# Row maxima as the exponential's bias, half products from chunk 8 on, and a new order, in a fused window-attention and gated-FFN kernel

## The chip, the cores and the metric

The kernel runs on one core of one Trainium2 chip. The metric is the device time of one launch in microseconds (us), as the median of three runs. Five engines work side by side, each through its own queue in order: TensorE (PE; its weight loads are listed apart, as PEld), VectorE (DVE), ScalarE (ACT), GpSimd (POOL), and SyncE (SP), which here only issues DMAs.

## The reference, cut to what matters

```python
# attention: 8 batches, 8 heads, 576 positions, 64 wide; key j counts for query i if 0 <= i - j < 64
scores = scale * np.matmul(q, k.transpose(0, 1, 3, 2))
scores = np.where(mask, scores, -1000000000.0)
scores = scores - np.max(scores, axis=-1, keepdims=True)
attn = np.exp(scores)
attn = attn / (np.sum(attn, axis=-1, keepdims=True) + 1e-09)
x = np.matmul(attn, v)              # then read as 4608 tokens of 512
# gated FFN: 512 -> 2048 -> 512
h = x @ w_in
sp = np.maximum(h, 0.0) + np.log1p(np.exp(-np.abs(h)))
out = (h * erf(sp)) @ w_out
```

## The kernel before

The 4,608 tokens are cut into 36 **units** of 128 tokens for the attention and 18 **chunks** of 256 tokens (two units each) for the FFN. Numbers are split into a high and a low float16 part, and a product is made of three float16 products (high·high, high·low, low·high).

**Attention of a unit** u. `s` (`scores`) makes the scores of all heads in PSUM, even heads in one bank, odd heads in the other ("parity" 0 and 1). `m` (`masked_max`) adds the mask and takes the row maxima, on DVE: four instructions of 128x128 for a parity, one for each head, each with an accumulator read that writes one column of `rmx`, a part of the tile `small`. `f` (`shift`) then subtracts the maxima from the 128x512 scores of the parity, on DVE or POOL; `e` (`expo`) takes the exponential on ACT, 128x512 at once from unit 6 on, with a constant bias; `ph` and `r` split it into high and low part, `t` transposes it by DMA, `a` multiplies by V on PE, `n` normalizes. Units 0 to 5 take another way through `tp` (a transpose on PE).

**FFN of a chunk** c. It is worked in two halves g (two numbers g for a chunk, from g = 2c). The first product is direct for chunks 0 to 3 (`mm`, line 763), and from chunk 4 on made of seven products of half-size blocks in place of eight (`M`, line 807), for which `U`, `Uh`, `Ul` (lines 791 and 797) prepare sums of weight blocks and `T`, `yh`, `yl` sums of x blocks. `E` and `C` bring the results from PSUM to the tile `h`; `sp`, `er`, `gt` are softplus, erf and the gate (`gt`: line 845, from chunk FAST on line 843). The second product is direct up to chunk FAST-1: `gh`, `gl` split the gated tile, `mA` and `mB` (`mm2`, line 869) multiply 128x512 at a time: per chunk 2 halves x 2 x 2 x 4 x 3 = 96 matmuls. From chunk FAST on it, too, is made of seven half products: `A` and `B` (lines 575/577 and 936) split a quadrant, `S` adds quadrants on an engine or by an accumulating DMA (lines 943 and 941), `P` and `Q` (`fast`, line 957) make 7 x 2 x 4 x 3 = 168 matmuls of 128x256 per chunk, `O` clears a bank, and `K` and `J` write the results out. Its weight sums are prepared once, by `Z`, `Yh`, `Yl` (lines 899 to 913).

**The order** is written out by hand: PLAN is one list of tokens (`m:7:0` is unit 7, parity 0; a letter at the end names the engine, v = DVE, a = ACT, g = POOL). The program issues them in that order, so each engine's queue is the list cut down to its tokens. FAST sets two more limits, LONE = FAST-3 and LENT = FAST-2, the chunks up to which some spare tiles serve another purpose.

Of the kernel before, what the change touches and what calls it, by code (L numbers as in the profile page):

```python
# [44 lines left out]
FAST = 7  # L45
# [236 lines left out]
def window_attention_gated_ffn(ctx, tc, q, k, v, w_in, w_out, masks, out):  # L282
# [6 lines left out]
    def fixed(name, shape, dt=F32):  # L289
        return const.tile(shape, dt, name=name)  # L290
# [778 lines left out]
```

## Time and profile before

| | |
|---|---|
| median of 3 runs | 837.74 us (837.42 to 838.18) |
| the profiled execution | 837.51 us, span of its instructions 835.6 us |
| mean granted TensorE clock | 0.998 |
| busy share of the span | PE 97%, PEld 81%, DVE 89%, ACT 76%, POOL 47% |

The span is the time from the first to the last instruction of the profiled execution; its own time is 1.9 us longer. A busy share says how much of the span an engine spent in instructions. Matmuls are pipelined, so that a busy PE is not a PE at its peak; a DVE or POOL instruction counts as busy also while it is held up by another engine.

### The profile page before, as it was taken

The numbers are of one execution on the slowest core, as the hardware profiler recorded it, in microseconds if no ns is written. First come the engines' busy times: TensorE is split into PE (matmuls) and PEld (weight loads), VectorE is DVE, ScalarE is ACT, GpSimd is POOL, SyncE is SP. The second block draws the span as 40 slices with busy tenths as digits, with TensorE's granted clock in tenths as the row PEclk, the third lists the DMA queues.
The fourth block names the chain that finished last, engine by engine and source line by source line (L and its number), as shares of the span: only waits on it lengthen the run. The fifth ranks groups of instructions, "written<-read, shape, count | busy, mean of one in ns | idle before, by whom it ended". The sixth has DMA issues, their size and how long they took to land.

```text
span 835.6 us, 26675 instructions
## 1 busy us (share of the span) xinstructions
PE 807.7 (97%) x11358; PEld 674.1 (81%) x11358; DVE 742.5 (89%) x1617; ACT 631.4 (76%) x833; POOL 396.8 (47%) x371
## 2 busy tenths in 40 slices
PE   7898989999999999999999999999999999999998
PEld 7786757656677775767889998989898989999997
DVE  5899999999998989889998989998879899887677
ACT  4798988778879888688758685868787858764673
POOL 1243445341644865353337367645554643723352
PEclk9999999999999999999999999999999999999999
DMA  9974485580476769162628595747774644522002
GB/s 351 361 279 166 127 218 147 101 196 2 108 162 163 151 144 179 46 153 51 120 49 176 113 179 102 157 89 180 118 153 96 154 90 91 90 49 61 9 5 73
DMA packets 148663, 109.87 MB, mean 131 GB/s; under 512 B 123456, under 2 KB 123840, under 8 KB 148544
## 3 DMA queue, kind: packets, MB, share of 16 engines
q1 hardware_dynamic: 145808, 98.60, 49.2%
q0 software_dynamic: 2592, 9.44, 6.3%
q8 instruction: 89, 1.46, 0.7%
q14 instruction: 30, 0.25, 0.1%
q10 hardware_dynamic: 144, 0.13, 0.0%
HBM read 59.64 MB, written 9.44 MB: 83 GB/s over the span
## 4 chain that ended last, share of the span: by engine, by line
PE 62%; DVE 24%; ACT 7%; issue 3%; POOL 2%; DMA 2%; DVEq 0%; SPq 0%; ACTq 0%; POOLq 0%
PE hp L807 23%; PE o L957 19%; PE o L869 11%; PE s L501 3%; PE hp L763 3%; PE av L557 2%; DVE y L845 2%; DVE y L843 2%; DVE w L421 2%; DVE h L936 1%; ACT y L831 1%; DVE vs L421 1%; DVE qk L512 1%; DVE h L823 1%; DVE sm L512 1%
## 5 line engine op out<-in xcount | busy, mean ns | idle before, releaser
L957 PEld LDWEIGHTS <-h 128*128 128x128 f16 x1632 | 155.8, 98 | 27.1 <-DVE h L936 5.6
L807 PE MATMUL hp<-arena,w 128*128 128x128 f16 x2688 | 162.4, 219 | 0.4 <-DVE h L823 0.4
L807 PEld LDWEIGHTS <-w 128*128 128x128 f16 x2688 | 154.8, 98 | 5.9 <-issue 1.2
L807 PE MATMUL hp<-arena 128*128 128x128 f16 x2016 | 119.7, 219 | 0.8 <-DVE h L823 0.7
L807 PEld LDWEIGHTS <-arena 128*128 128x128 f16 x2016 | 114.5, 98 | 4.0 <-issue 2.0
L957 PE MATMUL o<-w,h 128*128 128x256 f16 x912 | 108.8, 273 | 1.9 <-DVE h L936 1.3
L575 ACT ACTIVATE h<-hp 128x512 f32<-128x512 f32 x109 | 63.9, 588 | 42.9 <-PE hp L807 34.1
L763 PE MATMUL hp<-arena,w 128*128 128x256 f16 (+1 forms) x960 | 90.2, 252 | 2.1 <-DVE w L421 1.6
L936 POOL TENSOR_TENSOR h<-y,h 128x512 f16<-128x512 f32 x48 | 64.1, 1341 | 52.3 <-ACT h L575 20.5
L763 PEld LDWEIGHTS <-w 128*128 128x128 f16 x960 | 78.0, 98 | 13.4 <-DVE w L421 2.5
L831 ACT ACTIVATE y<-h,c 128x1024 f32<-128x1024 f32 x72 | 80.3, 1142 | 6.1 <-DVE h L823 4.4
L575 ACT ACTIVATE h<-y 128x512 f16<-128x512 f32 x84 | 50.1, 622 | 38.0 <-DVE y L943 14.6
L936 DVE TENSOR_TENSOR h<-y,h 128x512 f16<-128x512 f32 x88 | 70.2, 818 | 8.2 <-ACT h L575 4.2
L869 PE MATMUL o<-w,gh 128*128 128x512 f16 x320 | 74.7, 379 | 1.0 <-ACT gh L414 0.5
L838 ACT ACTIVATE y<-y 128x1024 f32<-128x1024 f32 x72 | 74.6, 1052 | 0.5
L823 DVE TENSOR_TENSOR h<-hp,h 128x512 f32<-128x512 f32 x84 | 57.6, 686 | 19.0 <-PE hp L807 14.7
L843 DVE SCALAR_TENSOR_TENSOR y<-h,small,y 128x1024 f32<-128x1024 f32 x44 | 58.2, 1327 | 4.3 <-ACT y L838 3.7
L869 PEld LDWEIGHTS <-gh 128*128 128x128 f16 x320 | 30.0, 98 | 34.2 <-issue 1.1
L957 PE MATMUL o<-spare,h 128*128 128x256 f16 x460 | 55.6, 273 | 1.0 <-DVE h L936 0.6
L838 ACT ACT_TABLE_LOAD x43 | 55.2, 1283 | 0.7
L517 POOL TENSOR_TENSOR sm<-sm,small 128x512 f32<-128x512 f32 x26 | 33.0, 1273 | 30.7 <-DVE small L512 21.4
L501 PE MATMUL s<-kr,qr 64*64 64x128 f32 x1152 | 40.7, 279 | 5.2 <-DMA kr<-k_in 4.7
(255 smaller groups left out, 1675.6 us busy)
## 6 DMA issues: line engine op xcount, KB each, us to landing
vr<-v_in SPq DMA_DIRECT2D x36, 520.0 KB, 4.4
kr<-k_in SPq DMA_DIRECT2D x36, 384.0 KB, 4.1
qr<-q_in SPq DMA_DIRECT2D x36, 256.0 KB, 4.0
y<-y POOLq DMA_DIRECT2D x18, 512.0 KB, 5.1
out<-ob SPq DMA_DIRECT2D x33, 256.0 KB, 3.3
w<-w_in SPq DMA_DIRECT2D x4, 1024.0 KB, 8.0
arena<-w_in SPq DMA_DIRECT2D x4, 1024.0 KB, 9.1
arena<-w_out SPq DMA_DIRECT2D x4, 1024.0 KB, 4.8
```

The source lines that it names most:

```text
L501: nc.tensor.matmul(sps[par][t, i, :], qx[rows, i, t], kx[rows, i, W * blk:W * blk + P], start=n == 0, stop=n == len(terms) - 1)
L517: eng_of(eng).tensor_tensor(s, s, m.unsqueeze(2).broadcast_to([P, HP, P]), op=ALU.subtract)
L575: nc.scalar.activation(dst, src, AF.Copy)
L763: nc.tensor.matmul(hps[pc % 2][:, f, at_t], w1[a][hf][:, cc, fs], xt[b][c % 2][:, cc:2 * NCC:NCC, :][:, at_x, :], start=(n == 0), stop=(n ...
L807: nc.tensor.matmul(bank[:, q, f, :], left(m, a, 2 * hf + q)[:, cc, f * P:(f + 1) * P], xt[b][c % 2][:, slot + cc, :], start=m in (1, 2, 5) ...
L823: nc.vector.tensor_tensor(dst, bank_view(1), dst, op=ALU.add)
L831: nc.scalar.activation(at(yb, g, n), at(hb, g, n), AF.Softplus, scale=st_c[g][:, n:n + 1])
L838: nc.scalar.activation(y, y, AF.Erf)
L843: nc.vector.scalar_tensor_tensor(y, at(hb, g, n), gain(g, n), y, op0=ALU.mult, op1=ALU.mult)
L869: nc.tensor.matmul(ops[j], a[:, f // 2, j, f % 2, :], w2[b][:, hf * GF + n * GF // 2 + f, :], start=n == 0 and f == 0 and a is gh and b == ...
L936: eng_of(eng).tensor_tensor(lo, quadrant(m)[:, 512 * h:512 * (h + 1)], hi, op=ALU.subtract)
L957: nc.tensor.matmul(dst, a[:, at_f], right(m, n, 2 * h + f // 2)[:, f % 2], start=False, stop=f == 3 and (a is lo or n == 1), skip_group_ch ...
```

## The change

From unit 6 on `f` is gone. A new step `nb` (`max_bias`) turns both parities' maxima of a unit at once (128x8) into -max/8 + 14 ln 2, and `e` takes the raw masked scores with that as bias. The bias is one column for each head, so a parity's exponential is four instructions of 128x128. FAST goes from 7 to 8: chunk 7's second product is direct, and ten chunks are left on half products (LONE and LENT follow). The tile `small` grows from 68 to 84 columns. PLAN is a new list.

```diff
-FAST = 7
+FAST = 8
 LONE = FAST - 3
 LENT = FAST - 2
...
-    small = fixed("small", [P, 68])
+    small = fixed("small", [P, 84])
...
-    rmx = [few(HP) for _ in range(4)]
+    mxs, nmx = ([few(2 * HP) for _ in range(2)] for _ in range(2))
+    rmx = [mxs[i // 2][:, i % 2 * HP:i % 2 * HP + HP] for i in range(4)]
...
+    def max_bias(u, eng):
+        if eng == "a":
+            nc.scalar.activation(nmx[u % 2], mxs[u % 2], AF.Identity, bias=shift14, scale=-0.125)
+            return
+        eng_of(eng).tensor_scalar(nmx[u % 2], mxs[u % 2], -0.125, LN14, op0=ALU.mult, op1=ALU.add)
...
-        nc.scalar.activation(s, s, AF.Exp, bias=shift14, scale=0.125 if u >= LATE else es)
+        if u >= LATE:
+            for j in range(HP):
+                nc.scalar.activation(s[:, j, :], s[:, j, :], AF.Exp, bias=nmx[u % 2][:, HP * par + j:HP * par + j + 1], scale=0.125)
+            return
+        nc.scalar.activation(s, s, AF.Exp, bias=shift14, scale=es)
...
-    "ph:6:1:g m:7:0 c:13 r:6:1:v py:3 e:6:0 mm:2:2 pc:3 gl:0:1 ph:6:0:a vh:6:a t:6:0 d:13 r:6:0:v mB:0:1:0 vh:7:g t:6:1 "
+    "gt:0:1 h:6:a n:4 s:6 gh:0:1:a gl:0:0 a:5:0 c:13 a:5:1 xh:4:g m:6:1 mm:2:1 lv:7 xl:4:g m:6:0 l:11 nb:6:a e:6:0 l:7 "
```

Of the tokens, 60 `f` go (39 of them on POOL, 21 on DVE) and 30 `nb` come (13 on ACT, 9 on DVE, 8 on POOL); chunk 7 loses 14 each of `P`, `Q`, `A`, `B`, 4 `S`, 3 `K`, 3 `J` and 2 `O`, and gains 8 `mA`, 8 `mB`, 4 `gh`, 4 `gl` and 2 `fo`. Among the tokens that stay, engines are dealt anew: DVE takes 12 more `pk` (a maximum over 128x512), 5 more `E` and 6 more `Uh`, POOL takes 6 more `Z`, 7 more `ph` and 5 more `xl` but 11 fewer `B`. Counted over the whole program, POOL's instructions with two input tiles (TENSOR_TENSOR) go from 207 to 169; those that stand in the list ahead of chunk 4's first product from 42 to 29, and those from chunk 9's first product on from 105 to 78.

On ACT, around the exponentials of unit 6 (tiles sm0 and sm1; h is filled from PSUM between them, p is the high part), before:

```order
L838 ACTIVATE y1_108<-y1_108 128x1024
L537 ACT_TABLE_LOAD
L537 ACTIVATE sm1_96<-sm1_96,small_65 128x512
L575 ACTIVATE h0_105<-hp1_116 128x512
L652 ACTIVATE arena_61<-arena_61 128x1024
L537 ACTIVATE sm0_95<-sm0_95,small_65 128x512
L575 ACTIVATE p0_0_97<-sm0_95 128x512
```

and now (line 541 is `expo`, line 513 `nb`, line 581 the copies of line 575):

```order
L658 ACTIVATE arena_61<-arena_61 128x1024
L513 ACTIVATE small_65<-small_65 128x8
L541 ACTIVATE sm0_95<-sm0_95,small_65 128x128 x4
L581 ACTIVATE h0_105<-hp0_115 128x512
L541 ACTIVATE sm1_96<-sm1_96,small_65 128x128 x4
L581 ACTIVATE p0_0_97<-sm0_95 128x512
```

Each exponential is four instructions, and `nb` stands ahead of them.

On POOL, in the stretch of units 6 and 7, two steps `U` (line 791) and the subtractions (line 517) stood before:

```order
L418 TENSOR_SCALAR w1_01_100<-w2_0_103,small_65 128x2x512
L791 TENSOR_TENSOR misc_76<-w1_00_99 128x512
L791 TENSOR_TENSOR misc_76<-misc_76,w1_10_101 128x512
L517 TENSOR_TENSOR sm1_96<-sm1_96,small_65 128x512
L517 TENSOR_TENSOR sm0_95<-sm0_95,small_65 128x512
L577 CAST p0_0_97<-sm1_96 128x512
L418 TENSOR_SCALAR spare_89<-vr1_88,csc_67 128x16x64
```

These first two `U` now stand on DVE (line 797), among the low parts of the weights (line 417) and small scales:

```order
L417 SCALAR_TENSOR_TENSOR w2_1_104<-w1_01_100,small_65,w2_0_103 128x1024
L797 TENSOR_TENSOR misc_76<-w1_00_99 128x512
L417 SCALAR_TENSOR_TENSOR w2_1_104<-w1_11_102,small_65,w2_0_103 128x1024
L583 COPY h1_106<-hp0_115 128x512
L405 TENSOR_SCALAR csc_67<-cpw_66 128x3
L748 TENSOR_SCALAR c1_77<-small_65,cpw_66 128x2
L797 TENSOR_TENSOR misc_76<-misc_76,w1_10_101 128x512
```

The subtractions are gone from POOL there, and the two `U` moved to DVE.

On PE, chunk 7's second product began after a product `M` (line 807) with half products of 128x256:

```order
L807 LDWEIGHTS arena_61
L807 MATMUL hp0_115<-arena_61 128x128
L957 LDWEIGHTS h1_106
L957 MATMUL o0_117<-w2_0_103,h1_106 128x256
L957 LDWEIGHTS h1_106
L957 MATMUL o0_117<-w2_1_104,h1_106 128x256
```

and now ends, ahead of such a product (line 813), with direct ones of 128x512 (line 875):

```order
L875 LDWEIGHTS h1_106
L875 MATMUL o1_118<-w2_0_103,h1_106 128x512
L875 LDWEIGHTS h1_106
L875 MATMUL o1_118<-w2_1_104,h1_106 128x512
L813 LDWEIGHTS arena_61
L813 MATMUL hp0_115<-arena_61 128x128
```

Chunk 7 went from 168 narrow matmuls to 96 of twice the width.

## Rows read from the trace of the kernel before

**Rows 1.** The page: its first line, and the busy time of each engine.
```profile
span 835.6 us, 26675 instructions
PE 807.7 (97%) x11358; PEld 674.1 (81%) x11358; DVE 742.5 (89%) x1617; ACT 631.4 (76%) x833; POOL 396.8 (47%) x371
```

**Rows 2.** Busy time of each engine in three stretches, with its columns' line.
```profile
core 0: us, PE busy (x) PEld busy (x) DVE busy (x) ACT busy (x) POOL busy (x), PEclk, DMA share, GB/s
95.00:190.00 95.00, 90.22 (x974) 62.22 (x973) 92.19 (x222) 77.06 (x99) 43.85 (x38) 0.98 0.68 159
190.00:400.00 210.00, 208.42 (x2696) 147.36 (x2695) 192.24 (x435) 173.86 (x238) 103.71 (x85) 1.00 0.54 116
400.00:836.00 436.00, 426.13 (x6418) 394.79 (x6415) 376.44 (x707) 307.31 (x400) 217.28 (x206) 1.00 0.52 103
```

**Rows 3.** The chain that ended last, 95 to 190 us: start, length, instruction.
```profile
98.45 1.18 DVE arena L577
...
100.84 1.98 DVE y L845
...
104.57 1.14 DVE y L845
...
115.48 1.05 DVE cmx L406
...
141.53 0.94 DVE small L726
...
149.63 0.17 DVE cmx L406
```

**Rows 4.** The chain that ended last, two long pieces on PE after 190 us.
```profile
348.12 8.63 PE o L869 x40
...
719.07 10.48 PE o L957 x96
```

**Rows 5.** ACT's groups by shape: busy, mean ns of one, idle before.
```profile
L537 ACT ACTIVATE sm<-sm,small 128x512 f32<-128x512 f32 x31 | 21.9, 715 | 3.7 <-DVE sm L517 3.5
...
L414 ACT ACTIVATE ob<-o,sg 128x256 f32<-128x256 f32 x19 | 8.9, 470 | 20.0 <-PE o L957 18.3 <-DVE ob L977 1.7
L834 ACT ACTIVATE small<-small 128x1 f32<-128x1 f32 x36 | 7.2, 200 | 0.6
```

**Rows 6.** Line 517, the subtraction: shortest, median, longest, in ns.
```profile
L517 POOL TENSOR_TENSOR sm<-sm,small x26: 1037/1042/2022, 7.7 to 612.0; 128x512 f32<-128x512 f32 x26
...
L517 DVE TENSOR_TENSOR sm<-sm,small x13: 673/682/1096, 8.5 to 684.1; 128x512 f32<-128x512 f32 x13
```

**Rows 7.** DVE in order of time, two stretches: start, length, instruction.
```profile
100.76 2.06 DVE L845 TENSOR_TENSOR y<-h,y 128x1024 f32<-128x1024 f32 x1
...
182.04 0.68 DVE L517 TENSOR_TENSOR qk<-qk,small 128x512 f32<-128x512 f32 x1
...
186.90 1.64 DVE L517 TENSOR_TENSOR qk<-qk,small 128x512 f32<-128x512 f32 x1
```

**Rows 8.** POOL in order of time, beside those; idle before in brackets.
```profile
99.73 2.01 POOL L517 TENSOR_TENSOR spare<-spare,small 128x512 f32<-128x512 f32 x1
...
115.45 1.04 POOL L517 TENSOR_TENSOR qk<-qk,small 128x512 f32<-128x512 f32 x1 [2.47 <-DVE cmx L447]
...
185.93 2.06 POOL L791 TENSOR_TENSOR arena<-arena,w 128x512 f32<-128x512 f32 x1 [5.14 <-DVE arena L791]
```

**Rows 9.** Line 517 on POOL, from 95 to 190 us alone.
```profile
L517 POOL TENSOR_TENSOR sm<-sm,small x6: 1037/1042/1892, 97.5 to 177.8; 128x512 f32<-128x512 f32 x6
...
L517 POOL TENSOR_TENSOR qk<-qk,small x4: 1037/1042/1045, 115.5 to 147.6; 128x512 f32<-128x512 f32 x4
L517 POOL TENSOR_TENSOR spare<-spare,small x1: 2006/2006/2006, 99.7 to 99.7; 128x512 f32<-128x512 f32 x1
```

**Rows 10.** Line 791, the steps `U`, on DVE: shortest, median, longest.
```profile
L791 DVE TENSOR_TENSOR misc<-misc,w x9: 677/683/694, 123.3 to 246.8; 128x512 f32<-128x512 f32 x9
```

**Rows 11.** PE in order of time, in chunk 7's half products.
```profile
418.88 0.72 PE L957 MATMUL o<-gh,h 128*128 128x256 f16 x5 [1.72 <-DVE h L936]
```

**Rows 12.** PE's weight loads waiting, 420 to 836 us: total, times, longest.
```profile
PEld L957 <- DVE h L936: 3.3, 6, 1.1
PEld L957 <- DVE h L577: 1.7, 4, 0.6
...
PEld L957 <- ACT h L575: 0.9, 2, 0.7
```

More of the change, by code (lines that the diff above doesn't have):

```diff
@@ L1002, in window_attention_gated_ffn @@
         "qh": q_hi, "ql": q_lo, "kh": k_hi, "kl": k_lo, "vh": v_hi, "vl": v_lo, "s": scores, "m": masked_max,
-        "f": shift, "tp": upend, "e": expo, "ph": expo_hi, "r": expo_rest, "t": turn, "a": weigh, "n": normalize, "xp": x_up, "xh": x_hi, "xl": x_lo,
+        "f": shift, "nb": max_bias, "tp": upend, "e": expo, "ph": expo_hi, "r": expo_rest, "t": turn, "a": weigh, "n": normalize, "xp": x_up, "xh": x_hi, "xl": x_lo,
         "xt": x_turn, "T": x_sums, "yh": odd_hi, "yl": odd_lo, "yt": odd_turn, "U": sum_step, "Uh": sum_hi, "Ul": sum_lo, "M": product, "E": take, "C": join, "L": fetch, "d": low_bits, "c": rebias, "o": assemble,
```

433 rows, old and new, of the table PLAN are left out of this document.

## The prediction

> **What bounds the kernel now.** I read the page first. PE is busy for 97% of the span and DVE for 89%; ACT has a quarter of the span free and POOL half [rows 1]. That names PE, but an average hides stages, so the next view is the chain that ended last, read against the busy time by stretch. From 95 to 190 us the chain runs mostly from one DVE instruction to the next, and DVE is busy for 92.19 of these 95 us while PE has 4.8 us free [rows 2, 3]. From 190 to 400 us PE is busy for 208.42 of 210 us, and the chain is made of long PE pieces [rows 2, 4]. From 400 us to the end PE is free for 9.9 of 436 us, some 4 of them after its last matmul [rows 2]. So there are two regimes: DVE sets the pace for about a tenth of the run, then PE does, with small waits in the stage of the half products. Time is won or lost in three ways only: PE's own work anywhere after 190 us, DVE's pace before, and PE's small waits behind 400 us. All that PE waits for in 95 to 836 us is 4.8 + 1.6 + 9.9 = 16.3 us; no new order can win more than that.
>
> **PE's work: up.** Chunk 7's second product was 168 matmuls of 128x256; 96 in a row took 10.48 us, 0.109 each, so 18.3 us. It becomes 96 of 128x512; 40 took 8.63 us, 0.216 each, so 20.7 us [rows 4]. That is **+2.4 us** in the regime where PE is the bound, with nothing to hide it. The two bank clears that go are single small matmuls; I count them as nothing.
>
> **DVE's work: dealt out again, not less.** The 21 subtractions that leave DVE take 0.68 us each, 14 us [rows 6]. But DVE takes over 12 maxima of 128x512, 5 copies from PSUM and 6 casts from other engines; at the same 0.68 us these 23 are 16 us. Over the whole run I take that as even, and none of it counts in the PE regime. In the DVE regime there is something to count: until unit 12 every subtraction stood on POOL, so DVE loses none there, while two steps U come from POOL to DVE among the weights' low parts. At 0.683 us [rows 10] they are **+1.4 us** of DVE's queue. The bound below is nothing (if DVE happens to wait just there), the one above is these 1.4 us.
>
> **POOL's work: what it holds up.** 39 subtractions of at least 1.04 us, 41 us in all, leave POOL [rows 6], which is not a bound. But POOL holds DVE up. The gate at 100.76 us took 2.06 us and 1.98 of the chain, against 1.14 on the chain for the same instruction at 104.57 [rows 3, 7]: a subtraction ran on POOL from 99.73 to 101.74 [rows 8], and the gate ended about one own length after it. The small mask at 115.48 took 1.05 us against 0.17 at 149.63 [rows 3]; a subtraction on POOL ran from 115.45 to 116.49 [rows 8]. POOL ran 11 subtractions from 95 to 190 us [rows 9]; I find five DVE instructions held by them, the first at 98.45 and the last at 141.53 [rows 3], by 0.4 to 0.9 us against the shortest of their kind, 3.7 us in sum. All 11 go. In their place POOL has three more steps U ahead of chunk 4's first product; such a step held a DVE instruction for 0.96 us (1.64 against 0.68, at 186.90) [rows 7, 8]. With the share that was held before, five in eleven, three steps cost 3 x 5/11 x 0.9 = 1.2 us. I take 3.7 - 1.2 = **-2.5 us**; the bounds are nothing (POOL's other work slides into the free slots) and -3.7.
>
> The Trainium skill says the same of the cause (GPSIMD Engine Reference, Specifications): POOL's SBUF interfaces are shared with VectorE, with contention for DVE instructions that have two SBUF inputs or run in a two-port mode. The gate, with two inputs, agrees. The page gives no price; by it alone the sign of this term would be as above.
>
> **The first half products.** In chunk 7, where they begin, PE waits 1.72 us for a DVE split of line 936 [rows 11]; twelve weight-sum steps (Z, Yh, Yl) still stand in the list behind the first split A. With chunk 8 as the first, four do. I take the wait down by 8/12, **-1.1 us**; bounds 0 and -1.7.
>
> **The later half products.** Behind 420 us PE's loads wait 3.3 + 1.7 + 0.9 = 5.9 us for splits of quadrants [rows 12]. These are DVE and ACT instructions on short chains, and POOL's two-input instructions from chunk 9 on fall from 105 to 78, by 26%. If the waits fall alike: **-1.5 us**; bounds 0 and -3.
>
> **ACT.** One instruction of 128 columns doesn't stand in the trace. Bounds: the single column's 200 ns and the 256 columns' 470 ns; on the line from 1 column (200) to 512 (715) it is about 330 ns [rows 5]. I take 330, the exponential being the nearest row. Four are 1.3 us for 0.715, +0.6 us for each of 60 parities, +36 us of ACT (by the bounds +5 and +70). Some 70 other ACT instructions go to DVE and POOL; at 0.47 to 0.715 us each that is -33 to -50 us. So ACT stays near 631 us of 836, and costs nothing on the path; what covers it is its quarter of free time. The wait that is added: `nb` needs both parities' maxima, and on ACT copies of h from PSUM stand behind it, for which PE's next product waits. It takes the place of an exponential that waited for a subtraction; I set it at nothing.
>
> The Trainium skill speaks against this edit (ScalarE: Activation LUTs, What ACT_TABLE_LOAD costs): an ACTIVATE with a pointer bias takes about 280 ns + 0.833 ns a column, and successive ones overlap by 93. For 512 columns that is 706 ns, where the trace has 715. By it four of 128 take an estimated 1.27 us, +34 us for the run, and the sum would be the same.
>
> **Sum.** 2.4 + 1.4 - 2.5 - 1.1 - 1.5 = -1.3 us. The profiled execution took 837.5, 0.2 below the median: **836.2 us**, a hair faster, just inside the 0.2% (1.7 us) that a measurement of this kernel can tell from no change.
>
> **Rivals.**
> *Slower: POOL's place is taken.* The order fills POOL's free slots with other two-input work at just the moments when DVE sets the pace; DVE is held as before. For it: DVE has 92 of 95 us busy there and any POOL instruction can hit. Against it: 13 of 42 such instructions ahead of chunk 4 are gone. Without the two terms of relief the sum is 2.4 + 1.4 - 1.1 = +2.7, **840.2 us**. It decides from the point where less than 1 us of the 4 us of relief arrives.
> *Slower: ACT gets into the path.* A block of four exponentials holds ACT for 1.3 us, at the bound 1.9, while a copy of h from PSUM stands behind it. ACT is busy for 77 of 95 us in the DVE regime [rows 2]. If a tenth of 60 blocks makes PE wait for 0.7 us, that is 4 us on top: with half of the relief lost, about **842 us**.
> *Much faster: the new order has fewer waits overall.* POOL's two-input work falls by 18%, and the waits are 16.3 us. If half of them go, the sum is 2.4 - 8 = -5.6, **832 us**. For it: the waits are many and short, as collisions would make them. Against it: some 4 us of them are the end, where nothing changes.
> *No effect beyond PE's work.* If the waits are set by latencies of chains and not by collisions, only 2.4 - 1.1 remains: **838.8 us**, within 0.2%.
>
> **How the numbers follow.** Forecast 0.35 (half of it faster by over 0.2%, half within); much faster 0.25; no effect 0.10, within; POOL's place taken 0.22, all slower; ACT in the path 0.08, slower. With a little of the forecast's and of the no-effect case's spread falling on the slower side: faster 0.42, same 0.25, slower 0.33. The forecast's own range, from its bounds, is 833 to 839. The range for 8 in 10 reaches to the neighbouring cases and some way past their centres, 829 to 843.
>
> **What would show it.** In the profile after: chunk 7's second product at 0.216 us a matmul, PE's total up by about 2.4 us; DVE's gates in 95 to 190 us without any of 2 us; the exponentials of 128x128 near 330 ns; no wait of 1.7 us at the first half product; and PE's waits for splits under 5 us. I would be wrong if DVE instructions are held as long as before by POOL's other work, or if PE's waits in the new order stand at places that this one doesn't have.

## The result and the profile after

The changed kernel takes **827.88 us** (827.21 to 828.89, 4 runs) beside 837.58 us of the kernel before (837.09 to 838.18, 4 runs): a ratio of **0.9877**, 95% interval 0.9847 to 0.9906. The profiled execution took 827.4 us, its span 825.6. The forecast was 836.2 us with a range of 829 to 843: the sign was the likeliest one, the size was wrong by 8 us, and the time lies outside the range.

The page after, its first line and the busy time of each engine:

```profile
span 825.6 us, 26617 instructions
PE 806.0 (98%) x11284; PEld 665.3 (81%) x11284; DVE 726.5 (88%) x1633; ACT 625.6 (76%) x942; POOL 354.8 (43%) x355
```

Busy times by stretch, of the kernel after (the columns are those of [rows 2]; the stretches are cut by time, so the new kernel is further on in its work in the later ones):

```profile
0.00:95.00 95.00, 84.83 (x1294) 70.96 (x1295) 82.81 (x261) 74.85 (x105) 29.12 (x42) 1.00 0.73 272
95.00:190.00 95.00, 93.11 (x1041) 64.92 (x1040) 91.84 (x239) 83.41 (x149) 35.91 (x31) 1.00 0.70 163
190.00:400.00 210.00, 210.00 (x2761) 148.42 (x2759) 186.87 (x432) 168.54 (x262) 104.63 (x103) 1.00 0.55 122
400.00:440.00 40.00, 40.00 (x549) 31.16 (x550) 32.71 (x54) 30.94 (x42) 24.68 (x22) 1.00 0.39 78
440.00:840.00 400.00, 378.10 (x5656) 349.81 (x5648) 332.30 (x652) 267.82 (x387) 160.45 (x160) 1.00 0.48 96
```

and of the kernel before, the stretches that [rows 2] doesn't have:

```profile
0.00:95.00 95.00, 82.91 (x1278) 69.76 (x1279) 81.62 (x256) 73.17 (x98) 31.99 (x44) 1.00 0.72 269
400.00:440.00 40.00, 37.72 (x555) 34.99 (x553) 38.11 (x68) 27.18 (x38) 14.67 (x16) 1.00 0.49 86
440.00:840.00 400.00, 388.42 (x5867) 359.80 (x5864) 338.32 (x640) 280.13 (x363) 202.61 (x191) 1.00 0.51 104
```

PE's free time, the length of a stretch less PE's busy time in it: 12.1 us became 10.2 in the first 95 us, 4.8 became 1.9 from 95 to 190, 1.6 became nothing from 190 to 400, 2.3 became nothing from 400 to 440, and behind 440 it is 7.2 and 7.5 (to the end of each span). That is 8.3 us of the 10.0 by which the span shrank. Behind 440 us, half of the run, nothing was won. The other 1.7 us went out of PE's busy time, although PE has 2.4 us more to do: in 95 to 190 us the granted clock was 0.98 before and is 1.00 now, which is some 1.7 us by the rows below; the other 2.4 us of these 4.1 are in PE's busy time too, and the rows don't resolve them.

Where the clock fell, PE of the kernel before in order of time (idle before in brackets):

```profile
104.45 0.22 PE L668 MATMUL av<-ident,acc 128*1 128x128 bf16 x1
105.30 0.27 PE L668 MATMUL av<-ident,acc 128*1 128x128 bf16 x2 [0.63 <-ACT arena L662]
105.50 1.10 PE L501 MATMUL s<-kr,qr 64*64 64x128 f32 x32
108.15 0.16 PE L674 MATMUL av<-wtop,one 1*128 1x1 bf16 x1 [1.54 <-DVE wtop L671]
```

and the stretch behind it:

```profile
108.00:110.00 2.00, 1.85 (x51) 1.63 (x51) 1.76 (x11) 0.62 (x1) 1.92 (x3) 0.53 0.85 232
110.00:112.00 2.00, 2.00 (x13) 1.50 (x12) 1.93 (x11) 1.00 (x2) 1.88 (x3) 0.62 1.29 310
```

The gate that a POOL subtraction held up [rows 3, 7, 8] stands on DVE ahead of both waits: line 662 on ACT, for which PE waits 0.63 us, itself waited for the DVE instruction right behind the gate (line 656, at 102.75 us), and `wtop`, for which PE waits 1.54 us, is the sixth behind it. A second hold on the way to `wtop` is not by a subtraction: a scale of 128x2, 0.21 us at its shortest, took 1.08 us beside a split on POOL (DVE, then POOL):

```profile
106.83 1.08 DVE L742 TENSOR_SCALAR c<-small,cpw 128x2 f32<-128x2 f32 x1
```

```profile
106.22 1.67 POOL L418 TENSOR_SCALAR gh<-y,small 128x1024 f16<-128x1024 f32 x1 [4.48 <-PE av L668]
```

Behind these waits the clock was granted at half, 1.2 GHz, for some 3.4 us (0.53 and 0.62 of 2 us each), which loses 1.7 us of PE's work. The same two places in the kernel after:

```profile
99.95 0.27 PE L674 MATMUL av<-ident,acc 128*1 128x128 bf16 x2 [0.48 <-DVE acc L670]
100.16 1.10 PE L497 MATMUL s<-kr,qr 64*64 64x128 f32 x32
101.19 0.17 PE L680 MATMUL av<-wtop,one 1*128 1x1 bf16 x1
```

No wait for `wtop`, and the clock stays at 2.4 GHz. Most of the scatter of the kernel before goes with such falls: of its 87 runs beside the experiments, 26 had a mean granted clock of at least 0.999, median 835.7 us, and 61 a lower one, median 838.2. (Where the clock fell in these runs isn't on record.) Of eight runs of the kernel after (four of them are "after, again" below), six are of the first sort, median 827.7. So at full clock the change is worth 8.0 us.

### The profile page after: what moved, and what is told of

It is laid out like the page before. It is cut to its first block, busy times and chain, and to the rows that moved or that the text cites. A ratio compares the mean times of both kernels' runs of the same rounds, so it can differ in the third digit from the quotient of the medians.

```text
span 825.6 us, 26617 instructions
## 1 busy us (share of the span) xinstructions
PE 806.0 (98%) x11284; PEld 665.3 (81%) x11284; DVE 726.5 (88%) x1633; ACT 625.6 (76%) x942; POOL 354.8 (43%) x355
## 4 chain that ended last, share of the span: by engine, by line
PE 77%; DVE 15%; ACT 4%; DMA 2%; issue 1%; SPq 1%; POOL 0%; DVEq 0%; POOLq 0%
PE hp L813 29%; PE o L963 21%; PE o L875 16%; PE hp L769 4%; PE av L563 3%; PE s L497 3%; DVE w L417 1%; DMA arena<-w_in 1%; DVE gl L417 1%; DVE sm L508 1%; DVE arena L662 1%; DVE y L851 1%; ACT y L837 1%; DVE h L583 1%; DVE y L849 1%
## 5 line engine op out<-in xcount | busy, mean ns | idle before, releaser
L963 PEld LDWEIGHTS <-h 128*128 128x128 f16 x1464 | 139.7, 98 | 23.3 <-DVE h L583 3.2
L963 PE MATMUL o<-w,h 128*128 128x256 f16 x816 | 97.2, 273 | 1.5 <-DVE h L583 0.9
L875 PE MATMUL o<-w,gh 128*128 128x512 f16 x384 | 89.1, 379 | 0.0
L942 POOL TENSOR_TENSOR h<-y,h 128x512 f16<-128x512 f32 x39 | 50.1, 1323 | 42.1 <-DVE h L583 24.6
L875 PEld LDWEIGHTS <-gh 128*128 128x128 f16 x384 | 36.0, 98 | 39.1 <-issue 0.3
L942 DVE TENSOR_TENSOR h<-y,h 128x512 f16<-128x512 f32 x83 | 60.5, 754 | 1.8 <-PE o L963 0.5
L849 DVE SCALAR_TENSOR_TENSOR y<-h,small,y 128x1024 f32<-128x1024 f32 x40 | 53.6, 1346 | 5.4 <-ACT y L844 4.8
L581 ACT ACTIVATE h<-y 128x512 f16<-128x512 f32 x61 | 36.6, 623 | 27.6 <-DVE y L849 8.8
L963 PE MATMUL o<-spare,h 128*128 128x256 f16 x414 | 49.5, 273 | 2.0 <-DVE h L583 1.4
L875 PE MATMUL o<-w,gl 128*128 128x512 f16 x192 | 47.4, 379 | 0.3 <-DVE gl L417 0.3
```

The source lines that it names most:

```text
L581: nc.scalar.activation(dst, src, AF.Copy)
L849: nc.vector.scalar_tensor_tensor(y, at(hb, g, n), gain(g, n), y, op0=ALU.mult, op1=ALU.mult)
L875: nc.tensor.matmul(ops[j], a[:, f // 2, j, f % 2, :], w2[b][:, hf * GF + n * GF // 2 + f, :], start=n == 0 and f == 0 and a is gh and b == ...
L942: eng_of(eng).tensor_tensor(lo, quadrant(m)[:, 512 * h:512 * (h + 1)], hi, op=ALU.subtract)
L963: nc.tensor.matmul(dst, a[:, at_f], right(m, n, 2 * h + f // 2)[:, f % 2], start=False, stop=f == 3 and (a is lo or n == 1), skip_group_ch ...
```

## The experiments

Each was run beside the kernel before on the same chip; those of one table group shared the chip. A **pass** is one subtraction `f` of a parity; the **old** and the **new** order, or list, are the PLAN of the kernel before and of the kernel after.

| group | kernel | median us | ratio, 95% interval |
|---|---|---|---|
| 1 | old order, no pass | 834.31 | 0.9959, 0.9932 to 0.9985 |
| 1 | old order, bias | 846.11 | 1.0107, 1.0064 to 1.0149 |
| 1 | new order, passes | 863.87 | 1.0305, 1.0266 to 1.0344 |
| 1 | new order, no maximum | 830.19 | 0.9898, 0.9863 to 0.9933 |
| 2 | after + 24 POOL adds, units 6 to 11 | 837.25 | 0.9993, 0.9980 to 1.0006 |
| 2 | after + 24 POOL adds, units 16 to 21 | 833.25 | 0.9955, 0.9939 to 0.9971 |
| 2 | old order, passes 6 to 11 gone | 834.12 | 0.9966, 0.9947 to 0.9985 |
| 2 | old order, passes 12 to 35 gone | 838.56 | 1.0003, 0.9984 to 1.0022 |
| 3 | old order, chunk 7 direct | 854.21 | 1.0198, 1.0166 to 1.0229 |
| 3 | old to 180 us, then new | 839.91 | 1.0025, 1.0005 to 1.0044 |
| 3 | new to 180 us, then old | 833.76 | 0.9959, 0.9934 to 0.9984 |
| 3 | old order, one-input passes | 833.90 | 0.9967, 0.9946 to 0.9989 |
| 4 | old to 210 us, then new | 833.96 | 0.9957, 0.9934 to 0.9979 |
| 4 | old to 385 us, then new | 831.43 | 0.9947, 0.9928 to 0.9966 |
| 4 | new to 360 us, then old | 834.98 | 0.9977, 0.9961 to 0.9994 |
| 4 | after, again | 828.23 | 0.9900, 0.9885 to 0.9914 |
| 5 | old order, tiny POOL steps | 834.12 | 0.9957, 0.9939 to 0.9975 |
| 5 | old order, passes 6 to 11 gone, again | 832.76 | 0.9941, 0.9921 to 0.9962 |

### Which part of the change: four kernels

The old order without any of the 60 passes (the exponential takes a constant, smaller bias, so the row maxima are not used):

```diff
-    "... m:6:1 d:12 mm:2:1 f:6:1:g n:5 er:1:1 f:6:0:g ..."
+    "... m:6:1 d:12 mm:2:1 n:5 er:1:1 ..."
-nc.scalar.activation(s, s, AF.Exp, bias=shift14, scale=0.125 if u >= LATE else es)
+nc.scalar.activation(s, s, AF.Exp, bias=shift9, scale=0.125)
```

> The kernel before with its old order and half products from chunk 7, but the 60 subtractions of units 6 to 35 left out and nothing in their place: the exponential takes the raw scores with one smaller constant bias, still 128x512 at once (the maxima are still computed, and not used). Theory A, the gain comes from POOL no longer holding DVE up in the stage where DVE sets the pace: the five holds by subtractions there, 3.7 us, go, and the time is 833 to 835 us. Rival B, the gain is the new list's own (better places for DVE's and PE's work, whatever POOL does): within 1.5 us of before, 836 to 838. Rival C, removing the passes is worth the whole gain in any order: 828 to 830.

The old order with `nb` at the place of each unit's later pass and four exponentials; chunk 7 stays in halves:

```diff
-    "... m:7:1 ... f:7:0:g e:7:1 ..."
+    "... m:7:1 ... nb:7:a e:7:1 ..."
```

> The old order and half products from chunk 7, with the edit of the exponential alone: the subtractions of units 6 to 35 go, the step nb stands in the place of the later one (engines as in the changed kernel), and the exponentials are four of 128x128 (three of them move behind nb). Theory A: as the run without any pass, at most 1 us more for nb and ACT's 0.8 us more for each parity: 833 to 836. Rival B: 836 to 839. Rival C: 828 to 830.

The new order and chunk 7 direct, each `nb` replaced by the unit's two passes on their old engines, one exponential of 512 columns:

```diff
-    "... m:6:0 l:11 nb:6:a e:6:0 l:7 ..."
+    "... m:6:0 l:11 f:6:0:g f:6:1:g e:6:0 l:7 ..."
```

> The changed kernel's order and half products from chunk 8, with the subtractions back: each nb is replaced by the unit's two subtractions on the engines that they had before (39 on POOL, 21 on DVE), and the exponential is one instruction of 128x512 again. Theory A: POOL's subtractions hold DVE again in the DVE stage, 3 to 7 us lost: 831 to 835. Rival B: the order keeps its gain, 828 to 829.5. Rival C: all is lost, 836 to 838.

The new order without `nb` and with one exponential of 512 columns at a constant bias (the row maxima are not used):

```diff
-    "... m:6:0 l:11 nb:6:a e:6:0 l:7 ..."
+    "... m:6:0 l:11 e:6:0 l:7 ..."
```

> The changed kernel without nb, and the exponential one instruction of 128x512 with a smaller constant bias on the raw scores (the maxima are computed and not used). All three theories: within 1 us of the changed kernel's 827.9, if ACT's four instructions for one cost nothing on the path, as the prediction had it. If ACT is in the path, 825 to 826.5.

Measured: 0.9959, 1.0107, 1.0305 and 0.9898. Leaving the passes out of the old order gives 3.4 us, no more. Beside the kernel before, the bias put into the old order by hand loses 9 us, and the passes put into the new order lose 26; both lie outside everything that was expected. The last kernel stands about where the kernel after does (0.9877 and, in a second run, 0.9900): `nb` and four exponentials for one cost nothing that shows. So the list and the exponential are fitted to each other, and neither half alone can be priced by putting it into the other list. PE's waits from 95 to 836 us in the new order with passes show where such a misfit goes, into splits of the half products that come late on DVE and POOL:

```profile
PE o L961 <- DVE h L581: 6.3, 5, 4.6
PE av L449 <- DVE cmx L404: 4.9, 4, 2.8
PE o L961 <- POOL h L940: 4.9, 3, 3.6
PE o L961 <- POOL h L581: 3.5, 1, 3.5
```

### Where the passes cost time

The passes of units 6 to 11 alone left out of the old order (a constant bias for these units), which is where DVE sets the pace; and the complement, those of units 12 to 35:

```diff
-bias=shift14, scale=0.125 if u >= LATE else es)
+bias=shift9 if 6 <= u <= 11 else shift14, scale=0.125 if u >= LATE else es)
```

> The kernel before with the subtractions of units 6 to 11 alone left out (12 of 60, all on POOL; a constant bias for these units, so their row maxima are computed and not used). Theory A: the whole gain of leaving all 60 out (3.4 us in the first job) is here: ratio 0.995 to 0.997, 834 to 835.5 beside 838. Theory C (each pass that goes helps a little, wherever it stands): a fifth of it, 837. Theory B: no change.

> The kernel before with the subtractions of units 12 to 35 alone left out (48 of 60: 21 on DVE, 27 on POOL), the other half of the split. Theory A: no change, 837 to 838, since PE leads there and its waits are not the subtractions'. Theory C: four fifths of the gain of leaving all out, 835. Theory B: no change.

0.9966 and 1.0003. Twelve passes on POOL carry the whole gain of leaving passes out (0.9959 for all 60), the other 48, of which 27 stood on POOL, nothing that shows. A second run of the first kernel gave 0.9941:

> The old order without the passes of units 6 to 11, unchanged from its first run, as the end to measure from: ratio 0.9966 there, 833 to 835.5.

PE in that run, at the place shown above:

```profile
104.16 1.10 PE L502 MATMUL s<-kr,qr 64*64 64x128 f32 x32
105.90 0.16 PE L675 MATMUL av<-wtop,one 1*128 1x1 bf16 x1 [0.64 <-DVE wtop L672]
```

The wait for `wtop` is 0.64 us in place of 1.54, the wait of 0.63 us ahead of it is gone, and the clock isn't lowered there. The other hold, by the split, is still on the way to `wtop`:

```profile
104.57 1.09 DVE L743 TENSOR_SCALAR c<-small,cpw 128x2 f32<-128x2 f32 x1
```

### By what: the hold on DVE, or POOL's queue

The old order, with the 12 passes reading one tensor (a constant is taken off in place of the row maximum):

```diff
+        if 6 <= u < 12:
+            eng_of(eng).tensor_scalar(s, s, 1.0, -40.0 * math.log(2.0), op0=ALU.mult, op1=ALU.add)
+            return
         eng_of(eng).tensor_tensor(s, s, m.unsqueeze(2).broadcast_to([P, HP, P]), op=ALU.subtract)
```

> The kernel before, in which the 12 POOL subtractions of units 6 to 11 read one tensor in place of two (a constant is taken off, not the row maximum): POOL runs as many instructions in the same places, but none with two inputs. Theory A (two-input instructions of POOL hold DVE): most of the gain of leaving them out, 834 to 835.5. Theory D (POOL's queue: what stands behind a pass comes late): near the kernel before, 837 to 838.

0.9967, by the ratio as without them. But this didn't settle it, for a reason that the rows show: the passes last 0.62 to 1.49 us instead of 1.04 to 2.01, and one that reads a single tensor still holds DVE. On POOL and on DVE:

```profile
98.37 1.49 POOL L518 TENSOR_SCALAR spare<-spare 128x512 f32<-128x512 f32 x1
```

```profile
99.30 1.63 DVE L848 TENSOR_TENSOR y<-h,y 128x1024 f32<-128x1024 f32 x1
```

The gate ends 1.07 us after the pass (100.93 and 99.86), as it did in the kernel before, where the pass was longer (102.82 and 101.74) [rows 7, 8]. The hold is shorter, not gone: the four DVE instructions that these passes held from 95 to 190 us lost 1.8 us, where the four of the kernel before lost 3.3. At full clock (a mean of 0.999 or more) the kernel takes 833.6 us (8 runs), between 835.7 before and 832.7 without the passes. PE still waits 1.48 us for `wtop`, with no wait just ahead, and here the clock doesn't fall:

```profile
106.25 0.16 PE L677 MATMUL av<-wtop,one 1*128 1x1 bf16 x1 [1.48 <-DVE wtop L674]
```

So the second try, three tiny POOL steps on 2 columns in place of each pass:

```diff
+        if 6 <= u < 12:
+            for j in range(3):
+                eng_of(eng).tensor_scalar(s[:, j, :2], s[:, j, :2], 1.0, 0.0, op0=ALU.mult, op1=ALU.add)
+            return
```

> The kernel before, where each POOL subtraction of units 6 to 11 is replaced by three POOL instructions in place on 2 columns of the same tile (multiply by one, add nothing; the exponential takes a constant bias): POOL is held for 0.9 to 1.9 us a pass, as such small ones take 0.3 to 0.65 us, and the exponential waits for them as before, but no 128x512 is read. Theory A (the passes hold DVE): 833.5 to 835, as without the passes. Theory D (POOL's queue and the exponential behind it): 836.5 to 838, as before.

0.9957, beside 0.9941 without any step on the same chip. POOL is busy for 42.1 us from 95 to 190 us, nearly as in the kernel before (43.85, [rows 2]) and 8 us more than without passes:

```profile
95.00:190.00 95.00, 92.69 (x1005) 64.17 (x1003) 93.06 (x233) 81.20 (x107) 42.10 (x58) 1.00 0.64 157
```

and three of these steps, which take 3.44 us together, run right beside the gate (POOL, then DVE):

```profile
97.46 3.44 POOL L521 TENSOR_SCALAR spare<-spare 128x2 f32<-128x2 f32 x3
```

```profile
98.49 1.21 DVE L851 TENSOR_TENSOR y<-h,y 128x1024 f32<-128x1024 f32 x1
```

The gate takes no longer than its usual 1.2 us. Most of the triples take 0.5 to 0.6 us, about half of a pass, so POOL's queue is lighter than with the passes. As far as that goes, POOL steps in these places, and exponentials that wait for them, cost nothing that shows; a long POOL instruction that DVE must wait out does.

### What more work on POOL costs in the new list

The kernel after with 24 added POOL adds whose result nobody reads, in the stage where DVE leads and, as a control, where PE does:

```diff
+    def pool_extra():
+        nc.gpsimd.tensor_tensor(junk.bitcast(BF16).rearrange("p (a b) -> p a b", a=2), mask[:, :2, :], mask[:, 1:, :], op=ALU.add)
```

> The kernel after with 24 added GpSimd two-input adds of 128x256 bfloat16 whose result nobody reads, two behind each masked maximum of units 6 to 11, where DVE sets the pace. Theory A (POOL's two-input instructions hold DVE up and this costs the path where DVE leads): 11 subtractions held DVE for 3.7 us there, so 24 shorter ones cost 2 to 6 us against the kernel after (827.9): 830 to 834. Theory B (the new list's own placement, not what POOL does): 827 to 828.5, since POOL has 59 of 95 us free there.

> The control: the same 24 added GpSimd adds, but behind the masked maxima of units 16 to 21, where PE sets the pace and has almost no waits. Theory A: nothing to 1 us, 828 to 829, and clearly less than the twin in the DVE stage. Theory B: the same as the twin. If both cost the same several us, the place doesn't matter and POOL's load alone does.

Against 0.9900 for the kernel after (on the chip of group 4) they cost some 8 and 5 us. The order is as expected, the sizes aren't: the control should have been free. Each costs in its own stretch: in the first PE is free for 7.1 us from 95 to 190 us in place of 1.9, in the control for 4.3 us from 190 to 400 us in place of nothing. PE's waits in the control, 190 to 400 us, name another mechanism:

```profile
PE o L876 <- POOL gh L415: 1.8, 1, 1.8
```

A split on POOL came late behind the added work; `junk` is also written by ACT, which ties the two queues (POOL waited 9.3 us for ACT's `junk` in the control, and not in its twin). The pair shows that the new list has little slack on POOL in either place, and doesn't price the hold by itself.

### Where the rest lies: chunk 7, and lists joined

Chunk 7 direct in the old order, placed by hand where its half products stood (LONE and LENT keep their values):

```diff
-FAST = 7
+FAST = 8
-    "... M:16:2 st:6:1 ... M:16:6 A:7:1:0:a A:7:1:1:v ... P:7:1:1 ..."
+    "... M:16:2 mA:14:1:1 mB:14:1:1 mA:14:1:0 mB:14:1:0 st:6:1 ... M:16:7 mA:15:0:1 ..."
```

> The kernel before, all passes kept, in its old order, with chunk 7 done directly: its half products go and 32 instruction groups of the direct product stand, placed by hand, at the places where they stood. If PE's added work alone counts (2.4 us) and the wait at the first half products stays: 840. If the step of the prediction holds (2.4 - 1.1): 839. If the wait there, 3 us around 400 to 420 us in the profile before, goes whole: 837. Theory B (half of the gain is in the list around chunk 7): 834 or less.

1.0198, a miss of all expectations: the hand-placed steps made PE wait for copies of h on two engines (PE's waits, 390 to 450 us), so this run says nothing of the step itself.

```profile
PE hp L804 <- ACT h L572: 4.8, 3, 2.6
PE hp L804 <- DVE h L820: 4.7, 2, 2.9
```

Joined lists do better. The tokens of one list stand up to a place, and behind it those of the other that are still to be done; the place where they join is the seam. An old part at the front has no passes for units 6 to 11 and a constant bias there, the exponential goes with its list, and LONE and LENT are set to fit. In short:

```diff
-PLAN = old[:]
+PLAN = old[:n] + [t for t in new if t not in old[:n]]
```

> The old order without the passes of units 6 to 11 up to the first step of unit 12 (about 180 us), behind that the new order with the row maxima in the exponential and chunk 7 direct. By the sum over the stretches of the two profiles, PE's waits behind 200 us are 12.2 us before and 9.8 after, with 2.4 of PE's work added: so 834 (as the old order without these passes alone, 834.1). Theory B (the new list's later part carries the rest of the gain): 830 or less.

> The complement: the new order with the maxima in the exponential up to the first step of unit 12, behind that the old order with its passes and chunk 7 in halves. By the stretches, PE's waits up to 200 us are 21.9 us before and 14.6 after, and the clock's fall of 3.4 us at 119 us cost 1.7 more: 829 to 830. Theory B's later part: 834 or more here.

> The old order without the passes of units 6 to 11 up to the normalisation of unit 10 (some 210 us; the lists differ by few steps there), then the new order with the maxima in the exponential from unit 14 on and chunk 7 direct. Theory L (the new list's part behind 210 us carries the rest of the gain, and the wait at the seam of 180 us hid it): 828 to 830. By the sum over the stretches (4.9 us fewer waits behind 200 us, 2.4 us more work): 831.5. If the two halves only work together: 834 or more, without a single wait of several us at the seam.

> The same with the seam at 385 us, just ahead of chunk 7's second product; the exponential takes the maxima from unit 24 on. If the rest of the gain lies at the first half products and behind: as with the seam at 210 us, 829 to 832. If it lies in 210 to 385 us: 834 or a little more, for chunk 7's added work.

> The complement: the new order up to the second product of chunk 6's first layer (some 345 us in the profile after), then the old one with its passes from unit 22 on and chunk 7 in halves. If the gain lies at the first half products: 833 to 834, as with the seam at 180 us. If it lies in 200 to 360 us: 830 or less, below the kernel after plus 2.

> The kernel after, unchanged, on the chip of these runs: the ratio 0.9877 measured on the other one, 826 to 829.

A seam has a price of its own, and it must be read before the time is. The first one has a wait of 8.3 us in it (PE's waits, 155 to 180 us), behind which the clock is at half:

```profile
PE o L876 <- DVE gl L418: 8.3, 1, 8.3
```

```profile
165.00:170.00 5.00, 0.00 (x0) 0.00 (x0) 3.09 (x18) 4.92 (x6) 0.09 (x1) 0.55 0.00 0
170.00:175.00 5.00, 3.93 (x10) 1.45 (x11) 2.87 (x3) 0.00 (x0) 1.07 (x1) 0.50 0.00 0
```

The seams at 210 and 360 us have waits of 2.1 and 2.5 us; so these three times (839.91, 833.96 and 834.98 us; the first and the last lie outside what was expected) are upper bounds and decide little. The new list up to 180 us with the old one behind has no wait above 0.9 us at its seam; it, too, missed its 829 to 830 (833.76). At full clock it takes 831.7 us (4 runs), 4.0 below the kernel before. The seam at 385 us has no wait, and its time lies in the expected 829 to 832. At full clock, step by step:

| at full clock (0.999 or more) | runs | median us |
|---|---|---|
| kernel before | 26 | 835.7 |
| without the passes of units 6 to 11 | 6 | 832.7 |
| and the new list from 385 us on, chunk 7 direct | 3 | 830.7 |
| kernel after | 6 | 827.7 |

Three steps of 3, 2 and 3 us. By all runs the last one is the ratio 0.9900 against 0.9947 on one chip, their intervals apart; the middle one, 0.9947 against 0.9966 and 0.9941, doesn't show by all runs. What the middle one does is seen at once in 400 to 440 us, where PE of the joined list is never free:

```profile
400.00:440.00 40.00, 40.00 (x517) 30.21 (x516) 32.67 (x54) 28.78 (x40) 22.16 (x20) 1.00 0.37 89
```

Of the last step, one wait can be named. In the first 95 us PE of the kernel before waits for a low part on DVE:

```profile
PE o L869 <- DVE gl L421: 2.4, 1, 2.4
```

In runs of the old order it is 1.2 or 2.4 us; the new list doesn't have it. Between the two profiles (828.8 and 825.6 us of span) PE's free time differs by 1.6 us, all in the first 400 us, and its busy time by the other 1.6; which moves of the list do it stays open.

## Why the prediction was wrong, step by step

**PE's work, +2.4: as forecast per matmul, but not seen in the total.** PE's busy time, which I expected 2.4 us up, went from 807.7 to 806.0 us. With the clock full in both, the old list without the first passes has 805.4 us and the list joined at 385 us 807.6. Chunk 7's direct product runs at 5.18 us for 24, 0.216 each, in the chain:

```profile
393.73 5.18 PE o L875 x24
```

**POOL's hold on DVE: cause right, the gross size about right, the charge against it wrong.** One of my five held instructions, the one at 139.44 us, stood beside a step `r` on POOL (line 544) and not beside a pass; the other four were held for 3.3 us. I took 3.7 us for the subtractions, 1.2 off for three other steps, and +1.4 for two steps U on DVE: a net gain of 1.1. The passes alone measured 2.9 and 4.9 us in two runs. The list up to 180 us with its U steps on DVE and POOL gives 0.9959, no worse than the same passes left out of the old list (0.9966 and 0.9941): the two charges, 2.6 us, don't show in the time, though that list differs in more than these steps.

What I left out is POOL's other work, which held DVE for longer than the passes did. Take every DVE instruction that began in 95 to 190 us and ran for at least 0.3 us longer than the shortest of its operation and shape while POOL ran something: in the kernel before these are 13 with 9.5 us, in the old list without the first passes 10 with 7.2 us, in the kernel after 3 with 2.6 us (4 with 2.9 in its second profile). So the new list meets fewer of the other holds, where I had charged 1.2 us for more. Steps U still hold DVE in it; one of them on POOL, and the DVE instruction that it held, 0.68 us at its shortest:

```profile
185.87 1.54 POOL L797 TENSOR_TENSOR arena<-arena,w 128x512 f32<-128x512 f32 x1 [7.63 <-DVE arena L797]
```

```profile
186.31 1.65 DVE L797 TENSOR_TENSOR misc<-misc,w 128x512 f32<-128x512 f32 x1
```

Little of this reaches PE: without the first passes it is free for 2.3 us from 95 to 190 us, in the kernel after for 1.9.

```profile
95.00:190.00 95.00, 92.73 (x1006) 64.36 (x1004) 93.01 (x233) 81.34 (x107) 33.70 (x29) 1.00 0.63 158
```

Line 851's gates from 95 to 190 us (shortest, median, longest):

```profile
L851 DVE TENSOR_TENSOR y<-h,y x9: 1204/1218/1437, 96.2 to 188.8; 128x1024 f32<-128x1024 f32 x9
```

None of 2 us is left. What I didn't price at all is that the held gate stood ahead of two waits of PE, and that the clock fell behind them: 1.7 us in the profile of before. The granted clock of 0.98 stood in [rows 2], and I read past it.

The Trainium skill would have told more than the sentence I used: its page SBUF — State Buffer (SBUF: two separate sides) says that VectorE and GpSimd take the ports that they share as an exclusive lock for a whole instruction (a VectorE instruction with two SBUF inputs against a GpSimd one that reads SBUF, among others), and that the other blocks fully. The trace agrees with that: the gate ended about one own length, 1.08 and 1.07 us, after the pass in the kernel before and in the one with one-input passes.

**The first half products, -1.1: the right place, mis-sized.** The wait of 1.72 us [rows 11] is gone whole, and with it all 2.3 us of PE's free time from 400 to 440. The half products now begin at 444.3 us, with chunk 8, and the profile names no wait of PE from 400 to 520 us:

```profile
444.28 2.79 PE L963 MATMUL o<-w,h 128*128 128x256 f16 x24
```

My "8 of 12 steps" took a wait as proportional to the work queued ahead of it. A likely reading, which no run tests, is that nothing is left to wait for once that queue is short enough.

**The later half products, -1.5: wrong.** PE's weight loads wait for splits as long as before, 6.1 us by the lines below. [rows 12] have 5.9, and two lines of 0.3 us for POOL that they leave out make it 6.5; I had expected under 5. Of the kernel after, from 420 us on:

```profile
PEld L963 <- DVE h L583: 3.2, 4, 1.7
...
PEld L963 <- DVE h L942: 1.5, 4, 0.8
...
PEld L963 <- POOL h L942: 0.9, 3, 0.3
...
PEld L963 <- POOL h L583: 0.5, 1, 0.5
```

POOL's two-input work fell by a quarter there and nothing came of it, so these waits don't follow the collisions. The run without the passes of units 12 to 35 agrees.

**ACT, 0: right.** An exponential of 128 columns takes 388 ns, not the 330 that I put between the rows; it is inside the bounds. By the Trainium skill (ScalarE: Activation LUTs, What ACT_TABLE_LOAD costs), 280 ns + 0.833 a column, it is an estimated 387. ACT's groups by shape:

```profile
L541 ACT ACTIVATE sm<-sm,small 128x128 f32<-128x128 f32 x128 | 40.0, 388 | 5.0 <-DVE small L515 4.8
L541 ACT ACTIVATE qk<-qk,small 128x128 f32<-128x128 f32 x104 | 32.5, 388 | 5.5 <-POOL small L515 5.3
```

They overlap: 128 of them are busy for 40.0 us, 0.31 each, so four take 1.25. The kernel without `nb` and with one exponential is no faster (0.9898).

**The step that failed** is the sum itself: "All that PE waits for in 95 to 836 us is ... 16.3 us", and then single terms for the waits that I had found. It left out the first 95 us, where PE was free for 12.1 us and 1.9 of them went; it left out the clock, 1.7 us; and it priced the waits from 190 to 400 us at nothing, where all 1.6 us went. Of the terms that it had, the passes were charged down to a net 1.1 us and are worth 3.0 at full clock, and the first half products were sized at 1.1 where 2.3 went. In all PE's free time fell by 8.3 us. The rival "much faster" came nearest: it took half of the 16.3 us (15.8 in truth, as 836 us lies 0.4 behind the end of the span), and 6.4 of them did go, to 9.4; but it had the same two gaps, and so stopped at 832.

## What to carry to other kernels

Read the granted clock of every stretch beside PE's free time: a wait behind which the clock falls costs twice, and whether it falls can differ from run to run, so that the scatter of the old kernel is itself a hint of time to be won. Long POOL instructions beside DVE cost time here where DVE led (12 passes), and none that shows where PE led (the 27 later ones): find what stands behind the held instruction before counting collisions, and count the holds by all of POOL's work, not by the part that you change. A list that was fitted to a set of instructions can't be tested by swapping parts into it: join whole lists at a place where few steps differ, and look at the seam first.

## What the runs showed of the hardware

A one-input POOL pass over 128x512 held a two-input DVE instruction until it ended, as a two-input one did (the gate ended 1.07 and 1.08 us after them); it is only shorter, 0.62 us at its shortest beside 1.04. Small DVE instructions were held too: a scale of 128x2 took 1.08 us beside a one-input split of 128x1024. POOL steps on 2 columns didn't hold the gate: three of them in 3.44 us left it at 1.21. It was they that took longer, 1.17 us each, where the others take some 0.2 to 0.3 us:

```profile
L521 POOL TENSOR_SCALAR sm<-sm 128x2 f32<-128x2 f32 x15 | 4.0, 291 | 1.1 <-DVE small L514 1.0
L521 POOL TENSOR_SCALAR spare<-spare 128x2 f32<-128x2 f32 x3 | 3.4, 1171 | 0.0
...
L521 POOL TENSOR_SCALAR qk<-qk 128x2 f32<-128x2 f32 x12 | 2.2, 196 | 3.0 <-DVE small L514 2.9
```

So the short steps lost time beside the long DVE instructions and did the gate no harm.
